# A fused attention, SoLU layer and expert layer on one core: the first experts' weights prepared during the first layer, in buffers of their own

## The chip, the cores and the metric

The kernel runs on one core of one Trainium2 chip. The metric is the device time of one execution in microseconds (us), and the number compared is the median of several executions. Five engines take part, each with its own queue that it works through strictly in order: TensorE (PE in the profile, PEld its weight loads), VectorE (DVE), ScalarE (ACT), GpSimd (POOL) and SyncE (SP), which here issues all DMA transfers.

## What is computed

Three stages, one behind the other:

```python
def reference(q, k, v, w_in, w_out, g_ln, domain_probs, w1, w2):
    # q, k, v: [2, 8, 576, 64]; heads 0..3: window of 32, heads 4..7: window 32 with dilation 4
    x = attention(q, k, v, masks)                      # softmax over the window
    x = x.transpose(0, 2, 1, 3).reshape(1152, 512)
    h = x @ w_in                                       # [1152, 1024]
    solu = h * softmax(h)
    ln = (solu - mean) / sqrt(var + 1e-6) * g_ln
    x = ln @ w_out                                     # [1152, 512]
    p = domain_probs / (domain_probs.sum(-1) + 1e-9)
    out = 0
    for e in range(4):
        out += p[:, e:e+1] * (relu(x @ w1[e]) @ w2[e]) # w1[e]: [512, 1024], w2[e]: [1024, 512]
    return out
```

`w_in` and `w_out` come as 64-bit floats and are converted to 32 bits on the chip.

## The kernel before

Every large product is made of three passes over operands that are split into a high and a low part (hi*hi, hi*lo, lo*hi). A split is two steps: a copy that rounds (`hi`) and a subtraction (`lo`).

The work comes in generators, each of whose steps is one or a few instructions up to the next `yield`. `ORDER` is a written list of tokens; each token runs one step of its generator, so it fixes the place of every instruction in every engine's queue. A `+` behind a token sends a `copy` to VectorE instead of ScalarE and a `pick` to GpSimd instead of VectorE. The tokens:

- `UP.t.b`, `UD.t.b`: attention units (plain or dilated heads, third t of the sequence, batch b), twelve in all, of twelve steps: scores on TensorE (L258, L269), row maximum, subtraction, exp, row sum, reciprocal, product `pd` (L288), six transposes on TensorE (L294), copy `pt`, product with v on TensorE (L307, `po`), and the split of the result into `xhi` and `xlo` (L244).
- `VI.j`, `VO.j.t`: conversion of `w_in` and `w_out` (bit work on ScalarE, VectorE and one `add` that `pick` places, L194; then the split `wh`, `wl`).
- `H.t` (t = 0 to 8, tiles of 128 tokens): x @ w_in (L336) and the SoLU part on `e`: maximum, exp, product (L345), centring (L350).
- `T.t`: eight transposes (L364) of `e`, its square sum (L366), split into `hh` and `hl` for the next product.
- `X.c.d`: the product with `w_out` (L385) for chunk c of three tiles and half d, into `xf`.
- `WP.g`: `prep_w1`, the 14 splits and 4 sums that make seven weight operands for a Strassen form of the up-projection of half-expert g; `XQ.s`: `prep_x`, the same for the tokens (s = 0: 512 tokens, s = 1: 640); `WV.g`: `prep_w2`; `u.s`, `d.t`: the up- and down-projections of half-expert 0.
- `lI`, `lW`, `lV` and others issue loads; `endE`, `endA`, `endH`, `endX` close and open memory pools; `sc` (`scales`, L597 to L604) computes the scale of each token from `esq`: six short VectorE instructions with one power on GpSimd (L602) between them.

Behind `ORDER`, a loop over g = 1 to 7 runs the other half-experts with fixed rules; there `prep_w1(g + 1)` is spread over `up(1, g)`, four of its steps on VectorE and the other sums and `lo` parts on GpSimd.

Scores, transposes, `po` and the transposes of `T` all write PSUM tiles of tag `pa`, of which there are two buffers used in turn. So a TensorE step that takes a `pa` tile waits until the tile taken two steps earlier has been read out: a score tile by the subtraction, a transposed tile by `pt`, a `po` tile by `xlo`, a `T` tile by `hl`. `H` and `X` use two buffers `pm` in the same way.

Of the kernel before, what the change touches and what calls it, by code (L numbers as in the profile page):

```python
# [29 lines left out]
UP.1.0 UD.0.0 VI.2+ UP.0.1 VI.1 VI.1 UP.1.0 UP.0.1 UD.0.0 VI.3 UP.0.1 UD.0.0 UD.0.0 VI.3 H.0 UD.2.0 UP.1.0 UD.2.0 VI.3 VI.3 UP.1.0 UP.2.0 UD.0.1 UP.0.1  # L30
lO.0.1 UP.1.0 UP.2.0 H.1 lP.1.1 VI.3+ UD.1.1 UD.0.1 VI.2 misc H.1 UP.2.0+ VI.3 VI.3+ UP.0.1 VO.0.1 UD.0.1 UD.0.1 VI.2 VO.0.1 UD.2.0 H.0 VO.0.0 H.0
UD.0.1 UD.1.1 UP.0.1 UD.1.1 VO.0.0 UD.2.0 endE UP.2.0 UP.0.1 UD.1.1 UD.2.0 UP.0.1 UD.0.1 H.0 UP.2.0 VO.0.1 VO.0.0 H.1 UP.2.0 H.0 VO.0.0 lvp.0.1 H.1
UP.0.1 lvd.2.1 H.0 UD.0.1+ VO.0.1 UP.2.0 UP.2.0 H.0+ H.1 UP.0.1 VO.0.0+ T.0 lvd.0.1 UP.0.1+ UP.0.1 VO.0.1+ UD.1.1 VO.0.0 T.0 VO.0.0 lO.1.0 T.0 H.2
UD.2.1 lO.1.1 T.0 UD.2.1 VO.1.0 UD.2.1 UD.0.1 H.1 H.1 UD.0.1 UD.2.1 H.2 VO.1.0 UD.2.1 VO.1.0 UD.0.1 H.1+ UD.1.1 T.1 UD.0.1 VO.1.0 UD.1.1+ VO.0.1 VO.1.1
T.1 H.2 H.3 UD.0.1 lvd.1.1 UP.2.1 T.1+ T.1 VO.1.0+ UD.1.1 H.2 VO.1.0 H.3 lO.2.0 UD.2.1 VO.0.1 UD.1.1 UP.2.1 lvp.1.1 H.2 UD.2.1+ VO.1.1 UP.2.1 VO.1.0
VO.2.0 VO.1.1 UD.1.1 VO.1.1 H.2+ H.3 VO.1.1+ VO.2.0 T.2 UD.1.1 T.2 VO.2.0 H.3 VO.2.0 UD.1.1 lO.2.1 UP.2.1 H.3 VO.1.1 H.4 T.2 VO.2.1 VO.1.1 VO.2.1 T.2
VO.2.1 H.3+ UP.2.1 UP.1.1 UP.2.1 UD.2.1 H.4 lvp.2.1 UP.1.1 VO.2.0+ VO.2.0 H.4 VO.2.1 lO.3.0 X.0.1 UP.1.1 UP.1.1 VO.2.1 UD.2.1 H.4 VO.2.0 VO.2.1 UP.2.1+
VO.2.1 VO.3.0 UP.1.1 VO.3.0 UP.2.1 UD.2.1 UP.1.1 UP.2.1 lO.3.1 UP.1.1+ VO.3.0 UD.2.1 VO.3.1 VO.3.0 X.0.0 UP.1.1 VO.3.1 VO.3.1 UD.2.1 VO.3.0 VO.3.0
VO.3.1 VO.3.1 H.4 UP.2.1 VO.3.1 VO.3.0 VO.3.1 X.0.1 UP.2.1 UP.1.1 UP.2.1 UP.1.1 endA UP.1.1+ X.0.1 X.0.0 T.3 X.0.0+ H.5 UP.1.1 T.3 T.4 H.5 T.4 H.5 H.6
H.5 T.3 H.5 H.7 H.5+ H.6 T.4 T.3 H.6 H.6 T.5 T.5 T.4 H.7 H.8 H.6 T.5 H.7 T.6 T.6 H.7 T.5 T.6+ X.1.0 X.1.0 H.8 H.8 T.6 H.7+ H.8 H.8+ T.8 T.7 X.1.1 T.7  # L40
T.8 endH X.1.0 T.7 lW.0 sc X.1.1 T.8 T.7 XQ.0 WP.0 T.8 X.1.1 WP.0+ WP.0 XQ.0 XQ.0 WP.0 WP.0+ XQ.0 X.2.0 WP.0 X.2.1 XQ.0 XQ.0 XQ.0 XQ.0 X.2.0 XQ.0 XQ.0+
# [679 lines left out]
```

## Time and profile before

| | |
|---|---|
| median of 3 executions | 539.1 us (538.33 to 539.56) |
| the profiled execution's own time | 539.05 us |
| its span, first to last instruction | 537.2 us |
| TensorE busy | 520.5 us, 97% of the span |
| VectorE, ScalarE, GpSimd busy | 350.4, 199.2, 170.3 us |
| granted TensorE clock, mean | 1.000 (2.4 GHz) |

The time of an execution is some 1.9 us more than its span. Times in the rows below are counted from the start of the span. A busy TensorE need not be at its peak, since matmuls overlap and their ends are modelled.

### The profile page before, as it was taken

The page shows a single profiled execution, that of the slowest core. Times are in us where ns is not written, and L with a number is a line of the kernel's source. Part 1 is how long each engine was busy: PE and PEld are TensorE (multiplying, and loading weights), DVE is VectorE, ACT ScalarE, POOL GpSimd, SP SyncE. Part 2 cuts the span into 40 slices and gives each one's busy share as a digit, 9 for nine tenths or more (in the row PEclk, how much of TensorE's full clock was granted, in tenths as well). Part 3 has the DMA queues.
Part 4 walks back from the last instruction along what each step waited for, and adds up shares of the span by engine and source line. Part 5 has one row for each costly group of instructions (what it writes and reads, how often), then busy time and mean ns, then how long its engine had stood idle before and what let it go on. Part 6 is the DMA issues. An engine that isn't in the chain of part 4 may idle for free.

```text
span 537.2 us, 8748 instructions
## 1 busy us (share of the span) xinstructions
PE 520.5 (97%) x3660; PEld 466.1 (87%) x3660; DVE 350.4 (65%) x475; ACT 199.2 (37%) x302; POOL 170.3 (32%) x129
## 2 busy tenths in 40 slices
...
GB/s 292 326 291 100 61 129 10 0 1 1 79 88 109 118 2 0 159 0 1 79 79 1 1 156 1 0 91 69 1 1 158 0 1 78 1 1 0 2 78 99
DMA packets 20248, 35.79 MB, mean 67 GB/s; under 512 B 3568, under 2 KB 8368, under 8 KB 19824
## 3 DMA queue, kind: packets, MB, share of 16 engines
...
## 4 chain that ended last, share of the span: by engine, by line
PE 93%; DMA 2%; DVE 2%; ACT 1%; SPq 1%; issue 0%; DVEq 0%; ACTq 0%
PE pm L568 18%; PE pa L568 18%; PE pm L498 17%; PE pa L498 17%; PE pm L336 10%; PE pm L385 8%; PE pa L307 2%; DMA draw<-in_moe_w_in_dram 2%; PE pa L364 2%; PE pa L294 1%; DMA rw<-in_moe_w_dram 1%; PE pa L269 1%; ACT pt L172 0%; ACT e L366 0%; DVE sm L279 0%
## 5 line engine op out<-in xcount | busy, mean ns | idle before, releaser
L511 DVE SCALAR_TENSOR_TENSOR hl<-ct,hh 128x512 fp32r<-128x512 f32 (+1 forms) x64 | 61.5, 979 | 32.4 <-ACT hh L509 32.4
L509 ACT ACTIVATE hh<-ct 128x512 fp32r<-128x512 f32 (+1 forms) x64 | 42.2, 682 | 51.9 <-DVE ct L541 22.9
L568 PE MATMUL pm<-wh,hh 128*128 128x512 f32 (+1 forms) x148 | 56.9, 384 | 0.6 <-DVE xf L573 0.6
L498 PE MATMUL pa<-xoh,hl 128*128 128x256 f32 (+1 forms) x192 | 56.9, 296 | 0.0
L498 PE MATMUL pm<-xoh,hl 128*128 128x256 f32 (+1 forms) x192 | 56.8, 296 | 0.0
L498 PE MATMUL pm<-xol,hh 128*128 128x256 f32 (+1 forms) x192 | 56.8, 296 | 0.0
L498 PE MATMUL pa<-xol,hh 128*128 128x256 f32 (+1 forms) x192 | 56.8, 296 | 0.0
L568 PE MATMUL pm<-wl,hh 128*128 128x512 f32 (+1 forms) x148 | 56.8, 384 | 0.0
L498 PE MATMUL pm<-xoh,hh 128*128 128x256 f32 (+1 forms) x192 | 56.8, 296 | 0.0
L498 PE MATMUL pa<-xoh,hh 128*128 128x256 f32 (+1 forms) x192 | 56.8, 296 | 0.0
L568 PE MATMUL pm<-wh,hl 128*128 128x512 f32 (+1 forms) x148 | 56.7, 383 | 0.0
L568 PE MATMUL pa<-wl,hh 128*128 128x512 f32 x144 | 56.1, 390 | 0.0
L568 PE MATMUL pa<-wh,hh 128*128 128x512 f32 x144 | 56.1, 390 | 0.0
L568 PE MATMUL pa<-wh,hl 128*128 128x512 f32 x144 | 56.0, 389 | 0.0
L525 POOL TENSOR_TENSOR ct<-ct,ct 128x512 f32<-128x512 f32 (+1 forms) x15 | 22.4, 1492 | 78.8 <-ACT ct L523 78.8
L417 POOL TENSOR_TENSOR wl<-wl,wh 128x1024 fp32r<-128x1024 f32 x7 | 16.9, 2413 | 95.7 <-ACT wh L172 95.7
L573 DVE SCALAR_TENSOR_TENSOR xf<-pm,pr,xf 128x512 f32<-128x512 f32 (+1 forms) x33 | 24.1, 730 | 32.9 <-PE pm L568 32.9
L172 ACT CAST wh<-wl 128x1024 fp32r<-128x1024 f32 x16 | 16.9, 1053 | 71.0 <-PE pa L568 40.6
L573 DVE SCALAR_TENSOR_TENSOR xf<-pa,pr,xf 128x512 f32<-128x512 f32 x31 | 23.1, 746 | 29.4 <-PE pa L568 29.4
L498 PEld LDWEIGHTS pm<-xoh,hh 128*128 128x128 f32 x192 | 36.4, 190 | 0.3
L498 PEld LDWEIGHTS pm<-xol,hh 128*128 128x128 f32 x192 | 36.4, 190 | 0.3
L498 PEld LDWEIGHTS pa<-xoh,hh 128*128 128x128 f32 x192 | 36.4, 190 | 0.3
(183 smaller groups left out, 1258.0 us busy)
## 6 DMA issues: line engine op xcount, KB each, us to landing
...
```

The lines of the kernel that those rows point to most:

```text
L172: nc.scalar.copy(out, in_)
L307: nc.tensor.matmul(po[64 * row:64 * row + 64, 0, o:o + 96], lhsT=vv, rhs=pt[:, j, :, g, :], start=True, stop=True)
L336: nc.tensor.matmul(pm[:, n, :], lhsT=xx[:, kk, cols], rhs=ww["in", kk][:, 512 * n:512 * n + 512], start=(n_ == 0 and i < 2), stop=(n_ == K ...
L364: nc.tensor.transpose(pa[:, f // 4, (f % 4) * 128:(f % 4) * 128 + 128], e[:, f // 4, (f % 4) * 128:(f % 4) * 128 + 128], ident)
L385: nc.tensor.matmul(pm[:, dd, 0:CW], lhsT=w_, rhs=x_[:, f, :], start=(f == 0 and i == 0), stop=(f == KF - 1 and i == 2))
L417: pick().tensor_tensor(out=out, in0=a, in1=b, op=op)
L498: nc.tensor.matmul(ps[:, ff, 0:n], lhsT=a[:, kk, fc], rhs=b[:, kk, :], start=kk == 0 and m == 0, stop=kk == 1 and m == 2)
L509: nc.scalar.activation(out=hv, in_=src, func=AF.Relu)
L511: nc.vector.scalar_tensor_tensor(out=lv, in0=src, scalar=0.0, in1=hv.bitcast(F32), op0=ALU.max, op1=ALU.subtract)
L525: poolv().tensor_tensor(out=c12, in0=c21, in1=c22, op=ALU.add)
L568: nc.tensor.matmul(po[:, u, 0:dn], lhsT=h_[:, f, cols], rhs=w_, start=(f == 0 and i == 0), stop=(f == 3 and i == 2))
L573: nc.vector.scalar_tensor_tensor(out=acc[:, t, dc], in0=po[:, u, 0:dn], scalar=pr[:, t, e:e + 1], in1=acc[:, t, dc], op0=ALU.mult, op1=ALU ...
```

## The change

The operands of the first half-expert's up-weights get buffers of their own: five of the seven pairs and the raw tiles `rw` in a pool `w1p` that is opened at `endA`, the other two at `endX`. Before, they lay in the memory of the chunk tiles `hh`, `hl` and of a pool that is opened at `endH`. So `lW.0` and `WP.0` can now stand amid `H`. To find the room, three of the four sums of `prep_w1` are made in place in the raw weights, those of `prep_x` in two temporaries instead of four, and the 640-token hidden tiles move to where the chunk tiles were. In the loop, the two sums that now come first and the one behind the first split run as the first, second and fifth step. `NPM` and `NPO` are 0 and change nothing. `ORDER` is a new list altogether.

```diff
 ORDER = """
-lI.0 lP.0.0 VI.0 lD.0 VI.0 UP.0.0 VI.0 UD.0.0 VI.0 UP.0.0 UP.0.0 UD.0.0 lI.4 lP.1.0 VI.4 UP.0.0 UD.0.0 UP.0.0 lI.1 UP.0.0 UD.1.0 UD.1.0 lI.2 VI.0+
...
+lI.0 VI.0 lP.0.0 VI.0 UP.0.0 VI.0 VI.0 lD.0 UP.0.0 lI.4 UD.1.0 UP.0.0 VI.0+ UD.0.0 UD.1.0 UD.1.0 UP.0.0 lP.1.0 VI.4 UP.0.0 UD.1.0 UP.0.0 UP.0.0+ lI.1
...
-                r = xo["p"].tile([128, 1024], F32, name=f"rw{kh}", tag=f"rw{kh}")
+                r = w1p[0].tile([128, 1024], F32, name=f"rw{kh}", tag=f"rw{kh}")
...
     def prep_w1(g):
-        if not w1op:
-            t6 = [hpools[0].tile([128, 6, 2, 256], F32R, name=n, tag=n) for n in ("hh", "hl")]
-            t1 = [xo["p"].tile([128, 2, 256], F32R, name=n, tag=n) for n in ("w7h", "w7l")]
...
-        s1, s2, s3, s4 = (x[:, :, 0:256] for x in temps("sw"))
+        s1 = w1p[0].tile([128, 2, 256], F32, name="sm1", tag="sm1")
         tt(s1, a21, a22, ALU.add)
         yield
+        tt(a21, a11, a21, ALU.subtract)
+        yield
         yield from split(*w1op[0], a11)
-        tt(s2, s1, a11, ALU.subtract)
-        yield
-        yield from split(*w1op[5], s2)
+        tt(a11, s1, a11, ALU.subtract)
+        yield
+        yield from split(*w1op[5], a11)
         yield from split(*w1op[4], s1)
         yield from split(*w1op[1], a12)
-        tt(s3, a11, a21, ALU.subtract)
-        yield
-        yield from split(*w1op[6], s3)
-        tt(s4, a12, s2, ALU.subtract)
-        yield
-        yield from split(*w1op[2], s4)
+        yield from split(*w1op[6], a21)
+        tt(a12, a12, a11, ALU.subtract)
+        yield
+        yield from split(*w1op[2], a12)
         yield from split(*w1op[3], a22)
...
+        w1p.append(ctx.enter_context(tc.tile_pool(name="w1p", bufs=1, side="right")))
+        for i in (0, 5, 4, 1, 6):
+            w1op[i] = [w1p[0].tile([128, 2, 256], F32R, name=f"w1{x}{i}", tag=f"w1{x}{i}") for x in "hl"]
...
-    cnt_w = {0: 3, 5: 3, 4: 2, 1: 2, 6: 3, 2: 3, 3: 2}
+    cnt_w = {0: 4, 5: 3, 4: 2, 1: 2, 6: 2, 2: 3, 3: 2}
...
-            run(up(1, g), lambda i: steps(nw, cnt_w[i], (0, 3, 10, 13)) if nw else None)
+            run(up(1, g), lambda i: steps(nw, cnt_w[i], (0, 1, 4, 13)) if nw else None)
```

Line numbers in the changed kernel are 2 to 4 higher. Three places show what the new list does to the queues.

**Behind the fourth score tile.** TensorE's queue before, from the scores of `UP.1.0` on, without the weight loads and the mask matmuls (pd0 belongs to `UP.0.0`, pd2 to `UD.1.0`):

```order
L269 MATMUL pa_303<-kTp0_103,qTp0_106 32x64 x24
L269 MATMUL pa_340<-kTd0_104,qTd0_107 32x64 x24
L294 MATMUL pa_370<-ident_69,pd0_113 128x128 x6
L269 MATMUL pa_401<-kTp0_103,qTp0_106 32x64 x24
L294 MATMUL pa_430<-ident_69,pd2_115 128x128 x6
L307 MATMUL pa_444<-pt_387,vp_293 64x96 x8
L307 MATMUL pa_470<-pt_439,vd0_105 64x96 x8
```

and in the changed kernel (pd2 again `UD.1.0`):

```order
L271 MATMUL pa_295<-kTp0_103,qTp0_106 32x64 x24
L296 MATMUL pa_324<-ident_69,pd0_113 128x128 x6
L271 MATMUL pa_341<-kTd0_104,qTd0_107 32x64 x24
L296 MATMUL pa_386<-ident_69,pd2_115 128x128 x6
L271 MATMUL pa_406<-kTp0_103,qTp0_106 32x64 x24
L309 MATMUL pa_446<-pt_368,vp_334 64x96 x8
L296 MATMUL pa_456<-ident_69,pd1_114 128x128 x6
```

The transposes of `UP.0.0` now stand ahead of the scores of `UD.2.0`, those of `UD.1.0` ahead of the scores of `UP.2.0`, and those of `UD.0.0` (pd1) come before the `po` steps of the dilated heads.

**The `po` step of `UD.0.1`.** TensorE's queue before, from that step (pa_880) on; pa_891 is `T.1` and pm_908 is `H.3`:

```order
L307 MATMUL pa_880<-pt_862,vd1_110 64x96 x8
L364 MATMUL pa_891<-ident_69,e_772 128x128 x8
L336 MATMUL pm_908<-wh0_184,xhi_86 128x512 x2
L336 MATMUL pm_908<-wl0_185,xhi_86 128x512 x2
L336 MATMUL pm_908<-wh0_184,xlo_87 128x512 x2
L336 MATMUL pm_908<-wh1_378,xhi_86 128x512 x2
L336 MATMUL pm_908<-wl1_379,xhi_86 128x512 x2
```

and in the changed kernel, where pa_969 is that step, pa_981 the transposes of `UD.1.1`, pa_993 `T.2`, pa_1011 the `po` step of `UD.1.1` and pm_1029 `H.4`:

```order
L309 MATMUL pa_969<-pt_902,vd1_110 64x96 x8
L296 MATMUL pa_981<-ident_69,pd2_115 128x128 x6
L366 MATMUL pa_993<-ident_69,e_884 128x128 x8
L309 MATMUL pa_1011<-pt_989,vd1_110 64x96 x8
L338 MATMUL pm_1029<-wh0_182,xhi_86 128x512 x2
L338 MATMUL pm_1029<-wl0_183,xhi_86 128x512 x2
L338 MATMUL pm_1029<-wh0_182,xlo_87 128x512 x2
```

Two steps further on, the buffer of the `po` tile is taken again, now by `T.2` with only one short step between; before, six groups of matmuls of `H.3` lay ahead of the next step that takes it.

**Ahead of the last chunk.** VectorE's queue before, from the product of `H.8` (L345) to the `hl` of `T.8` (pa_1528); L597 to L604 is `sc`:

```order
L345 SCALAR_TENSOR_TENSOR e_1521,nsum_81<-e_1521,pm_1429 128x1024
L597 TENSOR_SCALAR esum_80<-esum_80 128x9
L598 RECIPROCAL nmx_79<-esum_80 128x9
L599 SCALAR_TENSOR_TENSOR esq_82<-esq_82,nmx_79 128x9
L600 TENSOR_TENSOR esq_82<-esq_82,nmx_79 128x9
L601 TENSOR_SCALAR esq_82<-esq_82 128x9
L603 SCALAR_TENSOR_TENSOR nmx_79<-nmx_79,esq_82 128x9
L604 TENSOR_TENSOR pr_76<-pr_76,nmx_79 128x36
L244 TENSOR_TENSOR hl_1458<-pa_1537,hh_1457 128x8x128
L417 TENSOR_TENSOR ct0_1620<-xf_1275 128x2x256
L417 TENSOR_TENSOR sw0_1629<-rw0_1582,rw1_1584 128x2x256
L244 TENSOR_TENSOR hl_1458<-pa_1528,hh_1457 128x8x128
```

and in the changed kernel, from the product of `H.8` (L347) to the `hl` of `T.8` (pa_1591):

```order
L347 SCALAR_TENSOR_TENSOR e_1518,nsum_81<-e_1518,pm_1452 128x1024
L352 TENSOR_SCALAR e_1518<-e_1518,nsum_81 128x1024
L246 TENSOR_TENSOR hl_1479<-pa_1522,hh_1478 128x8x128
L246 TENSOR_TENSOR hl_1479<-pa_1480,hh_1478 128x8x128
L419 TENSOR_TENSOR w1l5_1303<-rw0_1360,w1h5_1302 128x512
L172 COPY xf_1296<-pm_1491 128x2x384
L172 CAST w1h4_1304<-sm1_1402 128x512
L419 TENSOR_TENSOR ct0_1633<-xf_1296 128x2x256
L419 TENSOR_TENSOR w1l4_1305<-sm1_1402,w1h4_1304 128x512
L246 TENSOR_TENSOR hl_1479<-pa_1591,hh_1478 128x8x128
```

`sc` is no longer ahead of the last chunk's `hl` (it stands behind the parts of `XQ.0`, during `X.2`), and pieces of `WP.0`, an `xf` copy and the first sum of `XQ.0` have taken its place.

## Rows read from the trace of the kernel before

**Rows 1.** The page's first part: busy us, share of the span, instructions.

```profile
PE 520.5 (97%) x3660; PEld 466.1 (87%) x3660; DVE 350.4 (65%) x475; ACT 199.2 (37%) x302; POOL 170.3 (32%) x129
```

**Rows 2.** Busy time by stretch: us of stretch, then PE, PEld, DVE, ACT, POOL, clock.

```profile
16.00:24.00 8.00, 7.08 (x136) 5.31 (x135) 7.79 (x15) 5.67 (x9) 5.79 (x7) 1.00 0.95 282
24.00:40.00 16.00, 14.90 (x255) 10.84 (x250) 13.47 (x24) 12.90 (x19) 11.09 (x6) 1.00 0.90 307
...
100.00:141.00 41.00, 40.25 (x222) 36.49 (x219) 20.98 (x30) 19.87 (x29) 1.82 (x1) 1.00 0.07 26
220.00:300.00 80.00, 80.00 (x480) 72.96 (x479) 50.65 (x58) 23.98 (x38) 34.86 (x22) 1.00 0.14 48
```

**Rows 3.** The waits of TensorE: us in total, times, longest.

```profile
PE pa L269 <- DMA kTp<-in_kp_dram: 1.4, 1, 1.4
PE pa L269 <- DMA kTd<-in_kd_dram: 1.2, 1, 1.2
PE pa L294 <- DVE xlo L244: 0.9, 1, 0.9
PE pm L385 <- DVE hl L244: 0.7, 1, 0.7
```

**Rows 4.** Timeline of the front: start us, duration, engine, instruction, idle before.

```profile
14.80 0.95 PE L269 MATMUL pa<-kTp,qTp 64*32 64x64 f32 x48 [1.36 <-DMA kTp<-in_kp_dram]
...
16.02 1.79 POOL L288 TENSOR_TENSOR pd<-sm,st 128x384 f32<-128x384 f32 x2
...
17.75 1.51 PE L294 MATMUL pa<-ident,pd 128*128 128x128 f32 x6
```

**Rows 5.** Timeline around the po step of UD.0.1, and a group of transposes.

```profile
57.05 0.93 PE L307 MATMUL pa<-pt,vd 128*64 128x96 f32 x16
...
58.02 0.89 ACT L172 CAST xhi<-pa 128x384 fp32r<-128x384 f32 x1 [0.81 <-PE pa L307]
...
58.94 0.86 DVE L244 TENSOR_TENSOR xlo<-pa,xhi 128x384 fp32r<-128x384 f32 x1 [0.40 <-ACT xhi L172]
...
62.53 0.88 PE L294 MATMUL pa<-ident,pd 128*128 128x128 f32 x6
```

**Rows 6.** Timeline ahead of the last chunk's product.

```profile
134.74 1.82 POOL L602 TENSOR_TENSOR esq<-esq,mhalf 128x9 f32<-128x9 f32 x1 [52.76 <-ACT xf L172]
...
136.59 0.17 DVE L603 SCALAR_TENSOR_TENSOR nmx<-nmx,esq 128x9 f32<-128x9 f32 x1 [2.00 <-POOL esq L602]
...
139.67 1.22 DVE L244 TENSOR_TENSOR hl<-pa,hh 128x1024 fp32r<-128x1024 f32 x1
```

**Rows 7.** The waits of VectorE from 16 to 85 us, first and last of six.

```profile
DVE xlo L244 <- ACT xhi L172: 1.8, 2, 1.4
...
DVE st L277 <- PE pa L269: 0.2, 1, 0.2
```

**Rows 8.** VectorE's groups by shape from 16 to 90 us: busy us, mean ns.

```profile
L194 DVE CUSTOM_DVE_ANT_0 cva<-cvr,cva 128x1024 uint16<-128x1024 uint16 x3 | 2.1, 684 | 0.0
...
L288 DVE TENSOR_TENSOR pd<-sm,st 128x384 f32<-128x384 f32 x2 | 1.4, 705 | 0.0
...
L219 DVE TENSOR_TENSOR wl<-eva,wh 128x1024 fp32r<-128x1024 f32 x1 | 1.2, 1224 | 0.0
L170 DVE CAST hh<-pa 128x1024 fp32r<-128x1024 f32 x1 | 1.2, 1214 | 0.0
L170 DVE COPY pt<-pa 128x768 f32<-128x768 f32 x1 | 0.9, 914 | 0.0
L350 DVE TENSOR_SCALAR e<-e,nsum 128x1024 f32<-128x1024 f32 x1 | 0.7, 749 | 0.0
...
L170 DVE CAST xhi<-pa 128x384 fp32r<-128x384 f32 x1 | 0.5, 547 | 0.0
```

**Rows 9.** GpSimd's groups by shape: the add of the weight conversion.

```profile
L194 POOL TENSOR_TENSOR eva<-eva,draw 128x1024 uint32<-128x1024 uint32 x2 | 4.9, 2436 | 3.2 <-DVE eva L192 3.2
L194 POOL TENSOR_TENSOR cva<-cva,draw 128x1024 uint32<-128x1024 uint32 x1 | 3.3, 3299 | 2.9 <-issue 2.9
```

More of the change, by code (lines that the diff above doesn't have):

```diff
@@ L20 @@
 KORD = (0, 1, 2, 3)
+NPM = 0
+NPO = 0
 HCUT = (1, 1, 2, 2, 4, 2, 4, 4, 4)
@@ L30 @@
[L30 to L41, printed above, removed]
@@ new lines @@
+VO.3.1 VO.3.0 VO.3.1 VO.3.0 VO.3.1 UP.1.1 VO.3.1 X.0.1 UP.1.1 X.0.0 endA X.0.1+ H.5 X.0.0+ UP.2.1+ H.4+ UP.1.1 UP.2.1 UP.1.1 T.3 H.5 T.3 H.5 T.3+ lW.0
+H.5 T.4 T.3 H.6 T.4 H.5 WP.0+ T.4+ H.7 H.5 WP.0 H.6 T.5 H.6 H.6 T.5 T.4 H.7 T.5 H.7 H.6 H.8 T.5 T.6 WP.0 H.7 X.1.0 T.6 WP.0+ H.8 T.6+ H.7 T.7 WP.0+ H.8
+H.8 WP.0 T.7 T.7 H.8 X.1.1 T.7 T.6 X.1.0 WP.0 X.1.0+ T.8 T.8 endH WP.0+ X.1.1 XQ.0 WP.0 T.8 XQ.0 T.8 XQ.0+ X.2.0 X.1.1+ X.2.1 lV.0 XQ.0 XQ.0 XQ.0 XQ.0+
+XQ.0+ WP.0 endX sc WP.0 XQ.0+ WP.0+ WP.0 XQ.0+ XQ.0 XQ.0+ XQ.0+ X.2.0 XQ.1 XQ.1+ XQ.0 XQ.0+ X.2.1 WP.0+ XQ.0 XQ.1 u.0 u.0 u.0 WP.0 XQ.1 WP.0+ lW.1 WP.0
@@ L251, in att_U @@
     def att_U(quad, t, b):
-        ps = ptile(False)
+        ps = ptile(unit[quad, t, b] < NPM)
         if quad == "D":
@@ L298, in att_U @@
         yield
-        po = ptile(False)
+        po = ptile(unit[quad, t, b] < NPO)
         vt = None if quad == "D" else vps.pop((t, b))
@@ L466, in prep_x @@
         oh, ol = xo["h"], xo["l"]
-        t1, t2, t3, t4 = (z[:, :, 0:n] for z in temps("sw" if s else "ct"))
+        t1, t3 = (z[:, :, 0:n] for z in temps("sw" if s else "ct", 2))
         tt(t1, b12, x[:, 0:2, c1], ALU.subtract)
         yield
-        tt(t2, b22, t1, ALU.subtract)
+        yield from split(oh[:, 4, :, co], ol[:, 4, :, co], t1)
+        tt(t1, b22, t1, ALU.subtract)
         yield
         yield from split(*(z[:, 0:2, :, co].rearrange("p b k n -> p (b k) n") for z in (oh, ol)), x[:, :, c1])
-        yield from split(oh[:, 5, :, co], ol[:, 5, :, co], t2)
-        yield from split(oh[:, 4, :, co], ol[:, 4, :, co], t1)
+        yield from split(oh[:, 5, :, co], ol[:, 5, :, co], t1)
         tt(t3, b22, b12, ALU.subtract)
```

39 lines of the change are left out of this document (24 added, 15 removed).

## The prediction, on record before the changed kernel was run

> **What bounds the kernel now.** I read the page first: TensorE is busy for 97% of the span, VectorE for 65%, ScalarE and GpSimd for little more than a third [rows 1]. Since a busy share is an average over stages, the busy time by stretch comes next. From 220 us on TensorE has no idle time at all in the stretch shown, while VectorE works for 50.7 of 80 us and GpSimd for 34.9 [rows 2]. So behind the front nothing can be gained by moving work of other engines, and nothing is lost as long as each piece still arrives before TensorE wants it. Only the front is open: between 16 and 40 us TensorE is idle for 0.9 + 1.1 = 2.0 us, while VectorE is busy for 7.8 of 8 and 13.5 of 16 us; between 100 and 141 us it is idle for 0.75 us [rows 2]. The waits say what ends those idle times: two DMA landings of keys (1.4 and 1.2 us), one `xlo` of VectorE (0.9 us), and one `hl` of VectorE ahead of the last chunk's product (0.7 us) [rows 3]. The change keeps TensorE's instructions and their sizes, so its time is this TensorE work plus whatever waits the new order leaves or makes. What a measurement can tell from no change here is about 0.2%, 1.1 us.
>
> **What the change takes away.** The wait ahead of the last chunk has its cause on VectorE. `sc` stands there; its fifth short instruction waits 2.00 us for the power on GpSimd, which takes 1.82 us, and behind it in VectorE's queue lie two `hl` subtractions and two sums; the last `hl` starts at 139.67 and ends at 140.89, and `X.2.0` waits for it [rows 6]. In the new queue `sc` stands during `X.2` and the four other pieces that lie ahead of the last `hl` wait for no power and no DMA. VectorE has 20 of 41 us free in that stretch [rows 2]. So this wait goes. It shows as 0.7 us of idle time [rows 3]; the first matmul of `X.2.0` had already been issued, and its modelled end hides a little of the gap, so I take 0.8 us; the bounds are 0 (the last `hl` is as late as before, now behind pieces of `WP.0`) and 0.9.
>
> **What the change adds.** One wait follows from TensorE's queue alone. In the new order the `po` step of `UD.0.1` is followed by six transposes and then by `T.2`, which takes the same `pa` buffer again. The buffer is free when `xhi` and `xlo` have been made from it. Before, `po` starts at 57.05, `xhi` runs from 58.02 for 0.89 us, and `xlo` ends at 58.94 + 0.86 = 59.80, which is 2.75 us behind the start of `po` [rows 5]; it cost nothing there, because half of `H.3` lay ahead of the next step on that buffer. In the new queue TensorE has only the `po` step itself (0.93 us) and one group of transposes (0.88 us) to fill these 2.75 us [rows 5]. That leaves 0.94 us at least, and more since these durations overlap with what comes next: I take 1.2 us. The upper bound is 2.4 us, if VectorE, which has a `T.1` subtraction of 1.2 us [rows 6] ahead of this `xlo`, is late as well. Queued behind `T.2` are the next `po` step and `H.4`, so all of TensorE's later work shifts with it; in the stretches behind it TensorE has no idle time in which to get this back.
>
> **The front up to 40 us.** The loads are issued in the same order up to the first of `vp`, so the waits for the keys stay. Behind the scores of `UP.1.0`, which end at 14.80 + 0.95 = 15.75 [rows 4], the new order puts one group of transposes (1.5 us [rows 4]) and one score tile, then wants `pd` of `UD.1.0`. That `pd` needs its row sum and reciprocal on VectorE, which now come behind a maximum, a subtraction, a part of the conversion and another unit's sum, some 3.1 us in all, and then a turn on GpSimd behind the `pd` of `UD.0.0`, 0.9 us each (two in 1.79 us [rows 4]). That gives about 15.8 + 3.1 + 1.1 = 20 us for the transposes, where TensorE is ready at about 18.4: a wait of 1.6 us that is new. Further waits follow the pattern of `T.2`: the two dilated `po` steps stand back to back and the transposes behind them take the first one's buffer, about 1.1 us. Against this stand the idle times of before that the new order dissolves, 2.0 us [rows 2]. What is saved ahead of it, an exp that no longer lies behind a load of `w_in` and transposes that start 2 us earlier than 17.75 [rows 4], is worth a part of the new waits. Laid end to end with the durations of the rows, the new order reaches the last step of `H.0` some 0.3 us later than the old one. I take +0.4 us, between -2.0 (all idle time goes) and +1.4 (the new waits in full, 1.6 + 1.1 + 0.7 against 2.0).
>
> A row here bears on TensorE's clock: six transposes take 1.51 us at 17.75 [rows 4] but 0.88 us at 62.53 [rows 5], though the granted-clock column shows 1.00, the level of 2.4 GHz, for both stretches. So TensorE comes up to speed somewhere in the front. The Trainium skill ("TensorE: Matmul & The Clock Gate", Part 1) says that the throttled state is the default and that sustained activity lifts it; by that rule the new wait before 20 us could put the rise off. It would then cost what the rows at the two paces differ by, 0.6 us for each group of transposes that falls before the rise, as far as TensorE is not waiting anyway; I count that among the slower cases.
>
> **What costs nothing, and under which cover.** `WP.0` has the same 18 steps as before, only earlier and more of them on GpSimd; between 100 and 141 us VectorE is busy for 21.0, ScalarE for 19.9 and GpSimd for 1.8 of 41 us [rows 2], which is room for all of it. Its raw weights are loaded right after `endA`, when no other load is under way. In the loop the sums move within the same stretch and stay on VectorE; the second sum of a11 must now wait until GpSimd's `lo` of a11 is done, since it overwrites its source. VectorE has 29 of 80 us free there and GpSimd 45 [rows 2], and the product that needs the result comes a whole tile of down-projections later. Were that cover gone, each of seven rounds would pay one GpSimd subtraction, 1.5 us or so.
>
> **The sum.** -0.8 + 1.2 + 0.4 = +0.8 us on the profiled execution's 539.05 us: 539.8 us. The median shown is 539.1, so the profiled execution needs no correction.
>
> **Rivals.** *VectorE becomes late before 85 us (slower).* The new list loads VectorE more. Ahead of the `xlo` of `UD.2.1` it drops a `pt` (0.91), a `pd` of each kind (1.4 together), a `wl` (1.22), an `xhi` (0.55) and an `lh` (1.21), 5.3 us in all; it adds two whole conversion adds (2 x 2 x 0.68 = 2.7), two centrings (1.5), four dilated `xhi` (no such row on VectorE; between the plain one, 0.55, and ScalarE's 0.89, so 2.2 to 3.6), half a `wl` (0.6) and a `pd` (0.7), 7.7 to 9.1 us [rows 5, 8]. That is 2.4 to 3.8 us more. VectorE's own waits between 16 and 85 us, six rows from 1.8 down to 0.2 with 4.7 us in sum [rows 7], can swallow this, and that is why I count nothing. If they stay as they are, the tile is free 2.4 to 3.8 us later than before, which decides as soon as it exceeds some 1.5 us of slack plus the 1.6 us by which TensorE itself is later: up to 1.2 us more than forecast, 541.0 us.
>
> *The waits are shorter than I lay them (faster).* If the new front dissolves most of the 2.0 us, so that -1.6 stands in place of +0.4, with -0.8 and +1.2 as above, the kernel takes 537.9 us. For it speaks that most waits in the front are ended by engines that only had other work ahead in their queues. Against it speaks that VectorE has little idle time there [rows 2].
>
> *Nothing moves (no change).* The gain ahead of `X.2` is eaten by the wait of `T.2` and the front ends even: 539.1 to 539.5 us.
>
> *GpSimd is late in `u.1` (slower).* The new list gives GpSimd several parts of `XQ.1` there. Its add of 1024 columns takes 2.44 us twice and 3.30 us once [rows 9], so it can be stretched by a third. The lows of `XQ.1` arrive by my count 2 us ahead of the products that read them; a third more on some 12 us of queue takes 4 us, which with the waits between them would leave TensorE waiting about 1 us: 540.8 us. The Trainium skill ("SBUF — State Buffer", Who interferes with whom) says that a VectorE instruction with two SBUF inputs and a GpSimd instruction that reads SBUF block one another; the spread of those rows agrees with it.
>
> **Chances and range.** The forecast 0.46, with its own range from 539.3 to 540.4; it straddles the bound of 540.1, so two thirds of it count as no change. The slower cases (VectorE late, GpSimd late, a clock that rises later) 0.26; the faster case 0.18; nothing moves 0.10. That makes faster 0.18, no change 0.32 + 0.10 = 0.42, slower 0.26 + 0.14 = 0.40. The range that leaves two in ten out goes from just below the faster case to the far side of the slower ones, 537.7 to 542.0 us.
>
> **What would show it.** Right: TensorE has no wait at `X.2.0`; `T` waits once at about 67 us for `xlo`, for about 1 us; the transposes of `UD.1.0` wait for `pd` near 20 us; no waits behind 220 us. Wrong: waits of TensorE for VectorE around 85 us, or a wait in `u.1` for GpSimd, or a front that reaches `H.0`'s last step well before 41 us. The forecast fails as a whole if the loop shows any new wait, since that would be paid seven times.

## The result and the profile after

The changed kernel takes 545.3 us (median of 4, 542.9 to 546.7), the kernel before 538.8 us (median of 4): a ratio of 1.0121, 95% interval 1.0094 to 1.0148. I had forecast 539.8 us, with a range up to 542.0. Its profiled execution took 544.40 us, with a span of 542.6 us: 5.4 us more than the span of before.

The page's first part of the changed kernel (busy us, share of the span, instructions) answers to [rows 1]:

```profile
PE 520.9 (96%) x3660; PEld 466.9 (86%) x3660; DVE 364.0 (67%) x474; ACT 185.5 (34%) x286; POOL 192.5 (35%) x146
```

TensorE's busy time is the same to 0.4 us. VectorE and GpSimd are busy for 13.6 and 22 us more; that includes time in which an instruction of one stands blocked by the other, as the rows below show. The stretches of [rows 2] in the changed kernel, same columns (behind the clock stand the busy share of the DMA engines and their GB/s):

```profile
16.00:24.00 8.00, 6.53 (x127) 4.91 (x125) 7.42 (x14) 6.64 (x10) 5.37 (x5) 1.00 0.84 216
24.00:40.00 16.00, 11.70 (x172) 8.90 (x180) 14.84 (x21) 9.97 (x14) 7.45 (x5) 1.00 0.92 327
100.00:141.00 41.00, 41.00 (x225) 36.90 (x225) 26.46 (x32) 13.84 (x23) 3.85 (x3) 1.00 0.02 8
220.00:300.00 80.00, 80.00 (x492) 73.85 (x491) 52.89 (x56) 24.56 (x39) 37.54 (x24) 1.00 0.17 53
```

Between 16 and 40 us TensorE is now idle for 1.5 + 4.3 = 5.8 us instead of 2.0. From 100 to 141 us and from 220 to 300 us it is not idle. The waits of TensorE, as in [rows 3], all but the first and the last two:

```profile
PE pa L296 <- DVE sm L281: 1.7, 1, 1.7
PE pa L296 <- POOL pd L290: 1.3, 1, 1.3
PE pa L296 <- DVE xlo L246: 1.3, 1, 1.3
PE pm L338 <- DVE xlo L246: 1.3, 1, 1.3
PE pa L271 <- DMA kTp<-in_kp_dram: 1.1, 1, 1.1
PE pa L271 <- DMA kTd<-in_kd_dram: 1.0, 1, 1.0
PE pa L366 <- DVE xlo L246: 1.0, 1, 1.0
PE pm L497 <- DVE ct L540: 0.7, 1, 0.7
```

The two DMA waits are those of before, and the wait for `hl` ahead of the last chunk is gone. `pd` (19.6 us), `xlo` at L296 (31.9 us) and `xlo` at L366 (`T.2`, 70.3 us) were forecast. `sm` and `xlo` at L338 were not, and the wait for `ct` was only among the rivals, with another engine late. Some lengths below are counted from start to start: the time between the starts of two steps of TensorE, less what it is when nothing waits. They come out somewhat longer than the idle times of the list.

TensorE's milestones in the two traces say what each place costs. `H.4` begins at 72.19 instead of 67.81 us (+4.4; 1.2 of it is the wait at `T.2`, so 3.2 lie in the front). `X.2.0` begins at 144.31 instead of 139.86 (still +4.4), the first product of `u.0` at 160.95 instead of 157.52 (+3.4, so the last chunk gives back 1.0), and the second product behind `d.0` is under way at 197.97 instead of 192.60 (+5.4, so the stretch of `u.0` and `u.1` costs 1.9, of which 0.4 shows only in that second product, where TensorE waits for a last sum of `u.1`). It ends at +5.4.

What the unforeseen waits stand on is seen where VectorE's and GpSimd's rows lie beside one another. Timeline of the front of the changed kernel, in order of start: VectorE, GpSimd and the two steps of TensorE that waited (`...` marks cuts in the rows of VectorE and GpSimd):

```profile
20.24 1.30 POOL L196 TENSOR_TENSOR cva<-cva,draw 128x512 uint32<-128x512 uint32 x1 [0.67 <-DVE cva L194]
20.43 1.65 DVE L192 TENSOR_SCALAR eva<-eva 128x1024 uint32<-128x1024 uint32 x1 [0.27 <-ACT eva L190]
21.49 1.74 POOL L221 TENSOR_TENSOR wl<-cva,wh 128x512 fp32r<-128x512 f32 x1
22.00 0.55 DVE L286 TENSOR_REDUCE st<-sm 128x6 f32<-128x390 f32 x1
...
22.69 1.62 DVE L194 SCALAR_TENSOR_TENSOR eva<-draw,eva 128x1024 uint32<-128x1024 uint32 x1
...
24.88 0.56 DVE L281 TENSOR_TENSOR sm<-pa,st 128x384 f32<-128x384 f32 x1
...
25.59 0.85 PE L296 MATMUL pa<-ident,pd 128*128 128x128 f32 x6 [1.74 <-DVE sm L281]
...
33.31 1.21 DVE L194 SCALAR_TENSOR_TENSOR cva<-draw,cva 128x1024 uint32<-128x1024 uint32 x1
34.45 0.68 DVE L192 TENSOR_SCALAR eva<-eva 128x1024 uint32<-128x1024 uint32 x1
34.65 2.74 POOL L196 TENSOR_TENSOR cva<-cva,draw 128x1024 uint32<-128x1024 uint32 x1 [1.79 <-issue]
35.16 3.32 DVE L194 SCALAR_TENSOR_TENSOR eva<-draw,eva 128x1024 uint32<-128x1024 uint32 x1
...
38.40 0.54 DVE L246 TENSOR_TENSOR xlo<-pa,xhi 128x384 fp32r<-128x384 f32 x1
...
39.00 0.73 PE L338 MATMUL pm<-wh,xlo 128*128 128x512 f32 x2 [1.30 <-DVE xlo L246]
```

The same L194 on the same shape takes 1.21 us at 33.31 and 3.32 us at 35.16. The long one ends at 38.48, 1.09 us behind the end of GpSimd's add (34.65 + 2.74 = 37.39): it did nearly its whole work after that add. L192, 0.68 us when alone, ends at 22.08, 0.54 us behind the end of the add at 21.54. So these are not instructions that run slower side by side: one waits until the other is through. Not every VectorE instruction is blocked, though: the row sum L286 takes its usual 0.55 us at 22.00 while GpSimd's `wl` runs from 21.49 to 23.23. The `xlo` behind L194 is late, and TensorE waits for it.

At the change from `u.0` to `u.1` it is the same (timeline of the changed kernel; `...` marks cuts in any row):

```profile
169.90 1.87 POOL L419 TENSOR_TENSOR xol<-sw,xoh 128x640 fp32r<-128x640 f32 x1 [2.12 <-ACT xoh L174]
...
170.26 2.06 DVE L510 SCALAR_TENSOR_TENSOR hl<-ct,hh 128x512 fp32r<-128x512 f32 x1
...
171.73 2.83 POOL L419 TENSOR_TENSOR wl<-wl,wh 128x1024 fp32r<-128x1024 f32 x1
...
172.24 0.68 DVE L534 TENSOR_TENSOR ct<-pa,ct 128x512 f32<-128x512 f32 x1
...
172.95 2.17 DVE L536 TENSOR_TENSOR ct<-ct,ct 128x512 f32<-128x512 f32 x1
...
175.04 0.68 DVE L540 TENSOR_TENSOR ct<-pm,ct 128x512 f32<-128x512 f32 x1
...
175.77 0.41 PE L497 MATMUL pm<-xoh,w1h 128*128 128x320 f32 x1 [0.72 <-DVE ct L540]
```

The `hl` (0.69 us elsewhere) ends 0.55 us behind the end of `xol` on GpSimd, the sum at L536 0.56 us behind the end of `wl`. The sum at L534, which takes an input from PSUM, runs beside `wl` in 0.68 us. The two blocked instructions lose 2.9 us together, L540 releases its tile late, and TensorE waits.

### The profile page after: what moved, and what is told of

It reads as the page before. It is cut to its first block, busy times and chain, and to the rows that moved or that the text cites. A ratio compares the mean times of both kernels' runs of the same rounds, so it can differ in the third digit from the quotient of the medians.

```text
span 542.6 us, 8750 instructions
## 1 busy us (share of the span) xinstructions
PE 520.9 (96%) x3660; PEld 466.9 (86%) x3660; DVE 364.0 (67%) x474; ACT 185.5 (34%) x286; POOL 192.5 (35%) x146
## 4 chain that ended last, share of the span: by engine, by line
PE 86%; DVE 7%; DMA 2%; ACT 2%; issue 1%; POOL 1%; SPq 1%; DVEq 0%; POOLq 0%
PE pm L567 17%; PE pa L567 17%; PE pm L497 15%; PE pa L497 15%; PE pm L387 9%; PE pm L338 8%; DMA kTp<-in_kp_dram 2%; PE pa L366 2%; PE pa L309 1%; PE pa L296 1%; DVE eva L194 1%; DVE hl L510 1%; DVE xlo L246 1%; PE pa L271 1%; ACT hh L508 0%
## 5 line engine op out<-in xcount | busy, mean ns | idle before, releaser
L510 DVE SCALAR_TENSOR_TENSOR hl<-ct,hh 128x512 fp32r<-128x512 f32 (+1 forms) x64 | 66.9, 1063 | 40.1 <-ACT hh L508 40.1
L497 PE MATMUL pm<-xoh,w1h 128*128 128x320 f32 (+1 forms) x224 | 66.6, 297 | 0.9 <-DVE ct L540 0.7
L497 PE MATMUL pm<-xoh,w1l 128*128 128x320 f32 (+1 forms) x224 | 66.4, 296 | 0.0
L497 PE MATMUL pm<-xol,w1h 128*128 128x320 f32 (+1 forms) x224 | 66.4, 296 | 0.0
L497 PE MATMUL pa<-xoh,w1h 128*128 128x256 f32 (+1 forms) x224 | 66.2, 296 | 0.1
L497 PE MATMUL pa<-xol,w1h 128*128 128x256 f32 (+1 forms) x224 | 66.2, 296 | 0.0
L497 PE MATMUL pa<-xoh,w1l 128*128 128x256 f32 (+1 forms) x224 | 66.2, 295 | 0.0
L497 PEld LDWEIGHTS pm<-xoh,w1h 128*128 128x128 f32 x224 | 42.5, 190 | 1.7 <-DVE ct L540 1.0
L497 PEld LDWEIGHTS pa<-xoh,w1h 128*128 128x128 f32 x224 | 42.5, 190 | 0.7 <-issue 0.4
L497 PEld LDWEIGHTS pa<-xol,w1h 128*128 128x128 f32 x224 | 42.5, 190 | 0.3
L497 PEld LDWEIGHTS pm<-xol,w1h 128*128 128x128 f32 x224 | 42.5, 190 | 0.3
```

The lines of the kernel that those rows point to most:

```text
L497: nc.tensor.matmul(ps[:, ff, 0:n], lhsT=a[:, kk, fc], rhs=b[:, kk, :], start=kk == 0 and m == 0, stop=kk == 1 and m == 2)
L510: nc.vector.scalar_tensor_tensor(out=lv, in0=src, scalar=0.0, in1=hv.bitcast(F32), op0=ALU.max, op1=ALU.subtract)
```

## Experiments

The theory: some of VectorE's instructions that work from SBUF alone (here L192, L194, L510 and L536) and GpSimd's block one another for the whole of an instruction, and this, not the amount of work, makes VectorE late. The rival: VectorE has too much in its queue. Ratios below are to the kernel before on the same chip. e1 to e4 ran on one chip, so their times compare directly; the others ran on other chips, and against e1 they are compared by their ratios.

**e1, the changed kernel again.** No edit.

> The changed kernel once more, unchanged. If the new waits come from the order itself, the same four waits stand in this profile too (transposes at about 25.6 and 31.9 us, the last step of a product at about 39.0 us, the product of the first tokens at about 175.8 us), each within 0.3 us of its length. If they come from chance, they differ by more. The times of the four executions so far lie between 542.9 and 546.7 us, and the two longest show a mean granted clock of 0.994 and 0.997: if the clock makes this spread, times above 545.5 go with a clock below 1.000 again; if not, times and clocks are unrelated.

Measured: 545.72 us (543.02 to 546.58), 1.0120 (1.0101 to 1.0139). The four waits stand there again, each within 0.1 us from start to start. One thing is new in this profile: the granted clock. Its windows (columns as above):

```profile
24.00:27.00 3.00, 1.41 (x36) 1.12 (x39) 2.90 (x7) 0.71 (x2) 0.99 (x1) 0.97 1.07 374
27.00:29.00 2.00, 2.00 (x42) 1.58 (x28) 1.90 (x3) 2.00 (x3) 0.00 (x0) 0.50 0.99 380
29.00:31.00 2.00, 2.00 (x18) 1.27 (x18) 0.93 (x3) 0.32 (x1) 1.60 (x1) 0.69 1.08 398
31.00:34.00 3.00, 1.68 (x31) 1.52 (x27) 1.71 (x4) 2.64 (x5) 1.83 (x2) 1.00 1.01 400
```

Behind the wait that ends at 25.59 us the clock is 0.50, the level of 1.2 GHz, for some 3 us, and the transposes of 31.86 stand at 33.30: 1.4 us more. In the first profile the clock stayed at 1.00 behind the same wait. But the clock doesn't sort the executions: 545.61 and 545.82 us came with a mean of 1.000, and 545.24 with 0.997. So the order makes the waits, and this mean of the clock does not explain the spread. (The mean is blind to one thing, the start of the front; see "The clock" below.)

**e2, one add from GpSimd to VectorE.**

```diff
-UD.2.0 UP.1.0 UP.1.0 VI.3 VI.2+ UD.2.0
+UD.2.0 UP.1.0 UP.1.0 VI.3 VI.2 UD.2.0
```

> One add of the conversion of w_in (1024 columns, at 34.65 us) goes from GpSimd to VectorE. Theory (VectorE and GpSimd block one another for the whole of an instruction): the 'or' behind it takes 1.2 instead of 3.3 us, the xlo that ended the wait at 39.0 us starts at about 37.5 instead of 38.4 us although VectorE has 1.2 us more to do, that wait shrinks from 1.5 to about 0.5 us, and the kernel is about 0.9 us faster than the changed one. Rival (VectorE simply has too much queued there): the xlo starts 1.2 us later, at about 39.6 us, and the kernel is about 1.2 us slower than the changed one.

Measured: 544.28 us, 1.0091 (1.0072 to 1.0110), 1.4 us less than e1. The same place on VectorE (the add is now L196):

```profile
34.09 1.23 DVE L194 SCALAR_TENSOR_TENSOR cva<-draw,cva 128x1024 uint32<-128x1024 uint32 x1
35.22 0.70 DVE L192 TENSOR_SCALAR eva<-eva 128x1024 uint32<-128x1024 uint32 x1
35.81 1.24 DVE L196 CUSTOM_DVE_ANT_0 cva<-draw,cva 128x2048 uint16<-128x2048 uint16 x1
36.95 1.24 DVE L194 SCALAR_TENSOR_TENSOR eva<-draw,eva 128x1024 uint32<-128x1024 uint32 x1
38.09 0.57 DVE L246 TENSOR_TENSOR xlo<-pa,xhi 128x384 fp32r<-128x384 f32 x1
```

From the first L194 to `xlo` VectorE now needs 4.0 us instead of 5.1, with one instruction more in between. TensorE's wait falls from 1.5 to 0.4 us, counted from start to start. The `xlo` itself starts at 38.1 and not at the expected 37.5 us, since the clock falls in this profile too (0.50 from 26.5 to 29.9 us) and the whole stretch stands 0.8 us later. The theory holds; the rival would have made the stretch longer.

**e3, two lo subtractions from GpSimd to VectorE.**

```diff
-... u.0 WV.0 XQ.1 u.0+ u.0 XQ.1+ u.0 u.0 ... XQ.1 u.0 WV.0+
+... u.0 WV.0 XQ.1 u.0+ u.0 XQ.1 u.0 WV.0 u.0 ... XQ.1 u.0
```

> Two lo subtractions (of XQ.1 and of WV.0, 1.9 and 2.8 us on GpSimd beside the changed kernel's stretch from 170 to 175 us) go to VectorE, the second one behind the sum that releases the tile TensorE waits for. Theory (blocking for whole instructions): VectorE's hl and sum there take 0.7 instead of 2.1 and 2.2 us, the releasing sum starts at about 173.0 instead of 175.0 us although VectorE has 2.0 us more to do, the waits of 0.3 and 0.9 us at 173.1 and 175.8 us go, and the kernel is about 1.2 us faster than the changed one. Rival (VectorE is overloaded): the releasing sum starts 0.8 us later than before the edit, and what stands behind it 2 us later; the kernel is 0.8 to 2 us slower than the changed one.

Measured: 543.27 us, 1.0076 (1.0052 to 1.0101), 2.5 us less than e1. From the first product of `u.0` to behind `d.0` TensorE needs 35.6 us instead of 37.0 (before: 35.1), so 1.4 us is this edit's. The place on VectorE:

```profile
169.51 0.68 DVE L510 SCALAR_TENSOR_TENSOR hl<-ct,hh 128x512 fp32r<-128x512 f32 x1
170.11 0.68 DVE L534 TENSOR_TENSOR ct<-pa,ct 128x512 f32<-128x512 f32 x1
170.82 1.07 DVE L536 TENSOR_TENSOR ct<-ct,ct 128x512 f32<-128x512 f32 x1
171.81 0.81 DVE L419 TENSOR_TENSOR xol<-sw,xoh 128x640 fp32r<-128x640 f32 x1
172.55 0.68 DVE L540 TENSOR_TENSOR ct<-pm,ct 128x512 f32<-128x512 f32 x1
```

Although `xol` is now in VectorE's way, L540 comes 3.0 us behind the start of `hl`, not 4.8. The waits of 0.3, 0.9 and 0.3 us are gone; one of 0.5 us for `xol` is new. Another 0.8 us is chance in the front of this profile, which the edit does not touch:

```profile
20.56 0.69 DVE L192 TENSOR_SCALAR eva<-eva 128x1024 uint32<-128x1024 uint32 x1
20.57 1.83 POOL L196 TENSOR_TENSOR cva<-cva,draw 128x512 uint32<-128x512 uint32 x1 [0.91 <-DVE cva L194]
```

Here GpSimd's add starts just behind VectorE's L192. Now L192 takes 0.69 us and not 1.65, the add takes 1.83 and not 1.30, and the wait at about 25 us is 1.2 instead of 2.1 us. Which of the two starts first decides who is blocked. The queues are the same as in the changed kernel, so a queue that is too full cannot be the reason for those 0.9 us. What is left between 2.1 us (this profile against the first of the changed kernel) and 2.5 us (the medians) is not seen in any trace.

**e4, the front of before.** The tokens up to the first step of `H.2` in the order of before, the rest as changed.

> The tokens up to the first step of H.2 in the order of the kernel before, all that follows in the order of the changed kernel, on the changed code. If the loss is where the profiles show it (3.0 us by the last step of H.0, 1.4 us at T.2, 1.9 us in u.1, less 1.0 us ahead of the last chunk), this gives back the first 3.0 us: about 541.4 us beside the changed kernel's profiled 544.4, and TensorE reaches the first step of H.2 at about 49.7 us. Rival (the front's delay only moves the later waits, which lie against VectorE's queue): waits at T.2 and behind it grow by as much as the front gives back, and the time stays above 543.5 us.

Measured: 541.59 us, 1.0058 (1.0036 to 1.0080). TensorE reaches `H.2` at 49.72 us as was expected, and `H.4` at 69.27, 2.9 us earlier than in the changed kernel; the waits at `T.2` (1.2) and in `u.1` (0.5, 0.9, 0.3) stay about what they were. The loss of the front is the front's own, and what is behind it doesn't grow in return. By the medians the old front gives back more, 4.1 us against e1: five of these six executions have a mean clock of 0.999 or 1.000, so falls of the clock belong to the new front's loss as well.

**e5, the order of before on the changed code.**

> The order of the kernel before, on the code of the changed one (sums in place, buffers of their own, two temporaries, the loop's new rules). If the whole loss lies in the order, this runs like the kernel before, 538.9 us within 1.1 us, with the wait of 0.7 us ahead of the last chunk as before and none behind 200 us. Rival (the sums in place bind GpSimd and VectorE to one another in the loop): waits of TensorE behind 200 us, seven times over, and 1 us or more above the kernel before.

Measured: 541.33 us, 1.0043 (1.0027 to 1.0058). No wait behind 200 us, so the rival is wrong; but the theory's number is wrong too, by 2.4 us. In `u.0` TensorE waits 1.8 us for a `w1l` of `WP.0`, and the clock is at 0.50 behind it. The changed code with `WP.0` late is worse than the old code with its own order; it needs the earlier place that the new order gives it. In the changed kernel this wait isn't there.

**e6, cover for the wait at T.2.**

```diff
-... UP.2.1 H.3 UD.0.1 T.1 VO.2.0 VO.1.1+ UD.1.1 UD.0.1 UD.1.1 UD.0.1 UD.2.1 T.2
+... UP.2.1 UD.0.1 T.1 VO.2.0 VO.1.1+ UD.1.1 H.3 UD.0.1 UD.1.1 UD.0.1 UD.2.1 T.2
```

> The changed kernel with the second half of H.3 moved from ahead of the po step of UD.0.1 to ahead of T.2, so that it covers the time until xlo is made, as in the kernel before. Theory (the wait at T.2 is only lack of cover): the wait of 1.2 us at 70.3 us goes, the kernel is about 1.2 us faster than the changed one. Rival (VectorE is late there anyway): the wait comes back at the po step of UD.1.1 or at a later step of H.4, and the gain is under 0.5 us.

Measured: 548.42 us, 1.0164 (1.0146 to 1.0182), slower than the changed kernel by some 2.4 us (1.0164 against 1.0120 in e1), so the theory is wrong. The wait at `T.2` is gone and a longer one stands at the `po` step ahead of it:

```profile
68.98 0.55 DVE L281 TENSOR_TENSOR sm<-pa,st 128x384 f32<-128x384 f32 x1
...
69.64 1.57 PE L309 MATMUL pa<-pt,vd 128*64 128x96 f32 x16 [2.36 <-issue]
```

Its `pa` buffer holds the scores of `UP.2.1` until this `sm` has read them. The half of `H.3` had covered that. Behind this wait the clock is at 0.50 again (from 69.3 to 72.7 us; `po` takes 1.57 us where it took 0.93). One piece of matmuls can't cover two places, so the 1.2 us at `T.2` did not come back by moving this one; whether another piece could cover it was not tried.

**e7, only the scales moved, in the kernel before.**

```diff
-... lW.0 sc X.1.1 T.8 ...   ... endX ...
+... lW.0 X.1.1 T.8 ...      ... endX sc ...
```

> The kernel before with only the scales moved behind the opening of the last pool, as in the changed kernel. Theory (the wait ahead of the last chunk comes from the power on GpSimd that VectorE waits for): TensorE's wait of 0.7 us there goes and the kernel is 0.9 us faster than before, about 538.0 us. Rival (the last hl is late anyway, behind the sums of the next stage): the wait stays at 0.3 us or more, and the time within 0.4 us of the kernel before.

Measured: 543.51 us, 1.0086 (1.0071 to 1.0100): slower than before by 4.8 us. Neither theory nor rival foresaw that. VectorE ahead of the last chunk:

```profile
138.16 0.69 DVE L417 TENSOR_TENSOR sw<-rw,rw 128x512 f32<-128x512 f32 x1 [1.73 <-DMA rw<-in_moe_w_dram]
138.78 1.22 DVE L244 TENSOR_TENSOR hl<-pa,hh 128x1024 fp32r<-128x1024 f32 x1
```

The first sum of `WP.0` waits for its raw weights, and the `hl` behind it is as late as ever: TensorE still waits, 0.8 us. The trace of the kernel before already had this wait, in a line that [rows 6] leaves out (timeline of the kernel before):

```profile
139.06 0.69 DVE L417 TENSOR_TENSOR sw<-rw,rw 128x512 f32<-128x512 f32 x1 [0.34 <-DMA rw<-in_moe_w_dram]
```

The last `hl` of [rows 6], at 139.67, stands right behind it in the queue. The power's wait of 2.00 us was over at 136.59, so what held up the `hl` last was the DMA; the power's wait had only shortened what was seen of it to 0.34 us. And the scales, with 2.0 us of waiting for the power, now stand in a stretch where VectorE has nothing to spare, so that a `lo` of `WP.0` is late for `u.0`. The wait of TensorE, and the windows there (same columns as above):

```profile
PE pa L498 <- DVE hl L417: 3.0, 1, 3.0
```

```profile
168.00:170.00 2.00, 1.33 (x8) 1.33 (x9) 2.00 (x5) 1.51 (x2) 0.10 (x1) 0.82 0.00 0
170.00:172.00 2.00, 2.00 (x10) 2.00 (x9) 2.00 (x3) 0.63 (x1) 1.69 (x1) 0.50 0.00 0
172.00:174.00 2.00, 2.00 (x14) 2.00 (x13) 2.00 (x4) 1.11 (x2) 0.00 (x0) 0.83 0.00 0
```

**e8, front of before, cover at T.2 and u.1 together.** The edits of e4, e6 and e3, the `xol` one place earlier.

> The changed code with the front of the kernel before (up to the first step of H.2), the second half of H.3 ahead of T.2, and the two lo subtractions of u.0's stretch on VectorE (the one of XQ.1 now one place earlier, since it ended a wait of 0.5 us in the run before). Theory (all of the loss is in these three places, and the gain ahead of the last chunk is real): 1.0 us faster than the kernel before, about 537.9 us. Rival (the waits only move on to the next piece that is late): 539 us or more.

Measured: 542.18 us, 1.0066 (1.0054 to 1.0079). That is 3.5 us slower than the kernel before, where 1.0 us faster was expected. The cover of e6 fails here as there (TensorE waits 2.4 us ahead of `po`, with the clock at 0.50 behind it). In `u.1` only 0.3 us is left.

**e9, the order of before up to endA.** So the front and `T.2` as before, `WP.0` and the last chunk as changed, `u.1` as in e8.

> The changed code with the order of the kernel before up to endA (all of the attention and the first chunk of X), the order of the changed kernel behind it, and the two lo subtractions of u.0's stretch on VectorE. Theory (the losses are the front, T.2 and u.1, the gain is the wait ahead of the last chunk): no wait at T.2, none ahead of the last chunk, at most 0.4 us in u.1; 0.6 us faster than the kernel before, about 538.2 us. Rival (the first experts' weights prepared amid H and T make VectorE late at another place between 96 and 200 us): a new wait there, and the time of the kernel before or more.

Measured: 538.32 us, 0.9986 (0.9977 to 0.9995), the size that was expected. No wait at `T.2` or ahead of the last chunk, 0.3 us in `u.1`. With `WP.0` early, in buffers of its own, and without the other parts of the new order, the kernel gains 0.8 us. That the buffers are needed for it is not shown: e12 gains as much without them.

**e10, one blocked instruction out of the way.**

```diff
-VI.4 VI.2 VI.1 lvd.0.0 UP.2.0 UP.2.0 lI.3
+VI.4 VI.2 lvd.0.0 UP.2.0 UP.2.0 VI.1 lI.3
```

> The changed kernel with one VectorE instruction of the weight conversion (the 'or' of 1024 columns at 22.7 us, which GpSimd's lo subtraction blocked) put behind the maximum and the subtraction of UP.2.0. Theory (the granted clock falls behind TensorE's wait of about 2 us at 25.6 us): that wait shrinks from 2.1 to 0.5 us or less, the granted clock is 0.999 or more in every execution, and the median comes down by more than the wait, from 545.7 to about 543 us, with a narrower spread. Rival (the clock falls for reasons that lie outside this wait): means of 0.994 to 0.997 are still seen, and the median falls by 1.6 us at most.

Measured: 543.89 us, 1.0091 (1.0075 to 1.0107), some 1.6 us less than e1. The wait falls from 2.1 to 0.5 us, but 1.6 us come back one step on, where the scores of `UP.0.1` wait for a `pt`: they start 2.5 us behind the start of the transposes, in the changed kernel 0.8. In this profile 0.7 us of that is TensorE's pace, since the transposes at 24.33 us take 1.51 us and not 0.85. The mean clock is 0.997 in three of five executions, and two of these are the fastest. So the theory's number for the clock is wrong. The profiled execution is not among the three, so where their clock fell is not seen.

**e11, the edits of e10, e2 and e8's u.1 in the changed kernel.**

> The changed kernel with three edits together: the 'or' behind the subtraction of UP.2.0, the add of 1024 columns at 34.7 us on VectorE, and the two lo subtractions of u.0's stretch on VectorE. If the waits add up independently, the profile loses 1.6 + 1.0 + 1.5 us against the changed kernel's 544.4: about 540.3 us, with the waits at 19.6, about 30 and about 67 us left. If blocked time only moves between VectorE and GpSimd, the sum is smaller, 542 us or more.

Measured: 541.64 us, 1.0054 (1.0041 to 1.0067); the profiled execution 540.90, 3.5 us less than the changed kernel's. 4.1 was expected, and 1.0 us came back at the `pt` of e10. But not all of the 3.5 us are the edits': in this profile the keys land 0.8 us earlier (the scores behind them start at 13.79 instead of 14.57 us), and the transposes at 18.84 us already take 0.87 us where those at 19.62 took 1.54. The ratio against e1's gives 3.6 us. So the three edits add up in the main; how exactly, one profile doesn't show.

**e12, one sum of WP.0 one place later, in the kernel before.**

```diff
-... T.7 XQ.0 WP.0 T.8 X.1.1 ...
+... T.7 XQ.0 T.8 WP.0 X.1.1 ...
```

> The kernel before with the first sum of WP.0, which waits for the raw weights' DMA, put one place later on VectorE, behind the last hl; the scales stay where they are. Run e7 took the power's wait away and the last hl was as late as before, behind this sum, which then waited 1.7 us for the DMA. Theory (both waits stand ahead of the last hl, and the order's gain there needs this sum out of the way as well): the last hl ends at about 139.9 instead of 140.9 us, TensorE's wait of 0.7 us falls to 0.2 us or less, and the kernel is 0.5 to 0.9 us faster than before. Rival (the power alone is enough to make the hl late): the wait stays at 0.5 us or more and the time within 0.4 us of the kernel before.

Measured: 537.62 us, 0.9975 (0.9966 to 0.9985): the lowest median here, though its interval overlaps that of e9. VectorE there:

```profile
138.91 1.22 DVE L244 TENSOR_TENSOR hl<-pa,hh 128x1024 fp32r<-128x1024 f32 x1
140.04 0.68 DVE L417 TENSOR_TENSOR sw<-rw,rw 128x512 f32<-128x512 f32 x1
```

The scales still wait for their power at the old place, and TensorE has no wait ahead of the last chunk any more. Between its start and that of the first product of `u.0`, `X.2` takes 16.6 us instead of 17.7.

## Why the prediction was wrong, point by point

**The front: the step that failed.** I took +0.4 us, with an upper bound of +1.4 "the new waits in full, 1.6 + 1.1 + 0.7 against 2.0". It cost 3.2 us. The waits that I named are there: `pd` near 20 us with 1.3 in the list of waits for the 1.6 forecast, the transposes behind the two dilated `po` steps with 1.3 for 1.1. Not named were those at 25.6 us (1.7 in the list, 2.1 from start to start) and 39.0 us (1.3 and 1.5). I laid the queues end to end with durations that single rows show, and let VectorE and GpSimd run side by side. In the trace they exclude each other: L192 and L194 with 1.65, 1.62 and 3.32 us where I had 0.7 and 1.2. For the wait at 39.0 us e2 shows it, where more work on VectorE made it earlier; for the one at 25.6 us the front of e3 does, where the same queues with the other start order made it 0.9 us shorter. e4 puts the size of the whole at 2.9 us. So the bound was none: it held the waits of the order, but not the work that grows because two engines meet. One reading was wrong as well: the two DMA waits that I gave as ends of the idle time between 16 and 40 us lie ahead of 16 us, at 10.7 and 14.8.

**T.2.** Forecast 1.2 us and found 1.2 from start to start (1.0 in the list of waits), at 70.3 us instead of 67 because of the front. The working holds. My later idea that one piece of cover would bring it back doesn't (e6).

**Ahead of the last chunk.** Forecast -0.8, measured -1.0. The size came out, but not for the reason given: I wrote that the wait has its cause in `sc`. There were two waits one behind the other, for the power and for the DMA of the raw weights. The second ended last, and to move `sc` alone left the `hl` late (e7). The sum of `WP.0` behind the DMA was the one to move (e12). The change did that too, by loading these weights at `endA`, so the -1.0 is partly luck.

**In u.1.** I had this as a rival, with GpSimd late for its own products, stretched by a third, at 1.0 us. The place and the cause (VectorE and GpSimd hinder one another) were right; who is late and how much was not. VectorE waits for whole GpSimd instructions and loses 2.9 us on two of its own, and TensorE loses 1.9. The Trainium skill ("SBUF — State Buffer", Who interferes with whom) says that whoever issues first holds the shared ports for the whole instruction and the other blocks fully. The rows agree: the blocked instructions end 0.5 to 1.1 us behind the other's end. I had quoted this section for one queue and read it as a slowdown; it belonged into every sum in which both engines work from SBUF.

**VectorE late before 85 us.** Not seen: TensorE has no wait in the list between `T.2` and 170 us. That VectorE's own slack took the extra work, as the forecast counted, fits with it.

**The loop.** One new wait, 0.2 us at 197.6 us, for a sum of `u.1`, and it is not repeated: behind 200 us there is none, and TensorE's lag stays at 5.4 us from 198 us to the end. The sums in place cost nothing there, as forecast.

**The clock.** The forecast put a late rise among the slower cases. The clock column can't show the rise: in both kernels it reads 1.00 for all of the front, while six transposes take 1.51 us at 17.75 in the kernel before and 1.54 us at 19.62 in the changed one, and 0.85 us at 25.59. The traces' own records of the clock begin only at 23.3 us (before) and 24.0 us (changed), both with 1.00, and what lies ahead of the first record is counted as 1.00, in the mean too. By these records the rise came 0.7 us later, worth some 0.3 us by an estimate from the two paces. In other executions it comes elsewhere (in e10 the transposes still take 1.51 us at 24.33, in e11 0.87 us at 18.84), and no mean shows that.

What the forecast did not have is a second fall behind waits of some 2 to 3 us (e1, e5, e7), some 1.5 us each time. In the ten executions of the changed kernel the mean is 0.997 or less five times, in 56 of the kernel before it is never under 0.999. The median lies 0.9 us above the profiled execution. How much of that is the clock and how much the question which of two instructions starts first is open: no run separates them.

The sum as it was: 3.2 + 1.2 - 1.0 + 1.9 = 5.3 of the 5.4 us in the span. Against the forecast of 0.4 + 1.2 - 0.8 the front is off by 2.8 us, and `u.1`, which stood among the rivals and not in the sum, by 1.9.
